# A two-branch linear attention kernel: the low parts of the folded weights move to VectorE, the output weights are split in other places, and the second fold's transposes stand later

## The chip, the cores and the metric

The kernel runs on one core of a Trainium2 chip. The metric is the device time of one execution in microseconds; lower is better. The kernel before takes 364.24 us (median of three runs, 363.75 to 364.63). The core's engines are named as in the profile: PE (TensorE, matrix products), PEld (its weight loads), DVE (VectorE), ACT (ScalarE), POOL (GpSimd) and SP (SyncE, which here only issues transfers).

## The reference

Two attention branches A and B read the same input `x` (2048 tokens, 448 channels, 16 heads of 28), and a per-token gate mixes their outputs. Each branch has weights of its own. Cut to what matters:

```python
q, k, v = split(x @ wqkv)                       # per head, 28 wide
pq, pk = q @ w_phi[h], k @ w_phi[h]             # per head, 28x28
phi_q = concat([softmax(pq), softmax(-pq)])     # 56 features
phi_k = concat([softmax(pk), softmax(-pk)])
kv, z = phi_k.T @ v, phi_k.sum(tokens)
o = (phi_q @ kv) / (phi_q @ z + 1e-6)
branch = o @ wo
out = g * branch_A + (1 - g) * branch_B         # g = sigmoid(x @ gate_w)
```

## The kernel before

**Arithmetic.** All large products are float32 made of two float32r parts: a matrix w is kept as a high part (w rounded by a copy on ACT) and a low part (w minus the high part, a subtraction). A projection of 256 tokens is then 22 matmuls (`proj`, L221). The `w_phi` of each head is folded into the weights of q and k beforehand, so that one projection gives `pq` or `pk`.

**The fold of branch B.** `load_strips` brings the raw weights in, heads on partitions; `fold_strips(1, ...)` multiplies them on PE by `w_phi` (L182) into two PSUM tiles, transposes these on DVE (L186), stores them to a DRAM buffer `td` (four transfers, L188) and loads them back in the wanted layout (three transfers, L191 and L193). `high_folded` then makes the high part on ACT (L200) and `low_folded` the low part (L204), which was POOL's. It is done twice: for the k weights (staged in `wtb[1]`, result `wkb`), and for the q weights (staged in `ctr`, result `wka`, whose space A's k weights leave).

**The output weights.** `wo` of both branches is seven chunks, 0 to 6. `load_wo(c)` brings a chunk from a DRAM copy `wos` into one half of `wtb[0]` or `wtb[1]` (L455), `high_wo(c)` (ACT, L134) and `low_wo(c)` (POOL, L137) split it, and two transfers store the parts in `wod` (L464, L465), from which they come back much later. `wo_part(c)` says where a chunk is staged, and the table `WOS` at which step it is split.

**Order.** The order on each engine is the order in which the program is written: the engines run their own queues in order and wait for each other by semaphores. The first loop has eight steps u of 256 tokens and does A's k and v: a k projection; on DVE the sums of the step before (`k_sums`: L251, L252; the normalisation is POOL's, L260); `k_shift` (DVE L235 to L237, then POOL L238); a v projection, whose result ACT moves out (`v_out`, L268); the exponentials (`k_exp`, ACT L242); and `kv_acc(u - 1)` on PE (L285), which needs the normalised features of the step before. In between stand A's first q projections (`q_front`, DVE L312 and L314, through DRAM buffers `qd` to tiles `tq`; `q_exp0`, `q_min`, `q_exp1` on ACT L337, DVE L341 with POOL L345, ACT L352; `q_turn`, DVE L355), both folds of B and the splitting of `wo`. The second loop has eight steps u, each with one q projection, one k and one v projection of B, `num` (PE L367) and `kv_acc`; `a_turn` (DVE L568) takes the two PSUM tiles of `num` out. At its step 0, `gates` turns the gate sums into a sigmoid (ACT L558, DVE L559 and L560).

**PSUM.** `two_tile()` deals out three tiles in turn (`two0`, `two1`, `two2`), two of them to a fold or to `num`; a projection waits until the tile's last reader is done.

The end of the first loop's step, as it matters here:

```python
        if u == 5:
            low_folded(wtb[1], wk[1], nc.gpsimd)
            load_wo(2, 3, 6)
            ...
            wtqb = load_strips(mid.tile([P, 2048], F32, name="ctr"), wqt[1])
        if u > 1:
            kv_acc(u - 1)
```

Of the kernel before, what the change touches and what calls it, by code (L numbers as in the profile page):

```python
# [15 lines left out]
S, D, H, DH = 2048, 448, 16, 28  # L16
# [33 lines left out]
def hedgehog_mix(ctx: ExitStack, tc: tile.TileContext, xd, wv, wkt, wqt, wphi, wo, cmask, cpmask, out):  # L50


    nc = tc.nc
# [28 lines left out]
    wtb = [res.tile([P, 2048], F32, name=f"wtb{i}") for i in range(2)]  # L82
# [64 lines left out]
    def two_tile(i=None):  # L147
        if i is None:
            i = turn[0] = (turn[0] + 1) % 3
        return twos[i].tile([P, 2, 512], F32, name=f"two{i}")  # L150
# [23 lines left out]
            nc.sync.dma_start(w[HP * r:HP * r + DH, :, :D], s[r][:, :, :D])  # L174
        return dst

    def fold_strips(b, wt, i):
        w, t = wt.rearrange("p (g c) -> p g c", g=4), wt[:, :4 * D]
        ts = [two_tile(), two_tile()]
        for g in range(4):  # L180
            for r in range(4):
                nc.tensor.matmul(ts[r // 2][HP * g:HP * g + HP, r % 2, :D], wps[HP * r:HP * r + DH, b, g],  # L182
                                 w[HP * r:HP * r + DH, g, :D], start=True, stop=True)
        o = t.rearrange("p (j i w m) -> p i w j m", i=2, w=2, m=HP)
        for j, ps in enumerate(ts):
            nc.vector.transpose(o[:, j], ps[:, :, :D].rearrange("p w (j m) -> p w j m", m=HP))  # L186
        for g in range(4):
            nc.sync.dma_start(td[i][:, g * P:g * P + P].rearrange("(j t) x -> t j x", t=HP),  # L188
                              t[HP * g:HP * g + HP].rearrange("t (j x) -> t j x", x=P))
        d = wt.rearrange("p (c x) -> p c x", c=4)  # L190
        nc.sync.dma_start(d[:, :3], td[i][:384].rearrange("(c p) x -> p c x", p=P))  # L191
        for p in (0, 64):
            nc.sync.dma_start(d[p:p + 64, 3], td[i][384:])  # L193
# [4 lines left out]
    def high_folded(wt, dst):  # L198
        w, d = folded(wt, dst)
        nc.scalar.activation(d[0], w, AF.Copy)  # L200

    def low_folded(wt, dst, eng):
        w, d = folded(wt, dst)
        eng.tensor_tensor(d[1], w, d[0].bitcast(F32), OP.subtract)  # L204
# [7 lines left out]
    def proj(u, w, ps, order=None):  # L212
        n = w.shape[3]
        for i, j in order or [(i, j) for i in range(2) for j in range(11)]:
            if i is None:
                warm(j)
                continue
            t = 2 * u + i
            x, o = xg[t // 4], (t % 4) * P
            xc, k, wc = TERMS[j]  # L220
            nc.tensor.matmul(ps[:, i, :n], x[:, xc, o:o + P], w[:, k, wc], start=j == 0, stop=j == 10)  # L221
        return ps
# [66 lines left out]
    def state_copy(b):  # L289
        nc.scalar.activation(kvs[b][:, :, :, :DH], kvp[b].rearrange("p g s f -> p s g f"), AF.Copy)  # L290
# [57 lines left out]
    def q_min(k):  # L348
        q_rest(k, q_least(k))

    def q_exp1(k):
        nc.scalar.activation(eq[:, 1, :, :, :DH], eq[:, 1, :, :, :DH], AF.Exp)  # L352

    def q_turn(k):
        nc.vector.transpose(wtb[k % 2], eq.rearrange("p s a c f -> p (s a c f)"))  # L355
        eTs[k] = wtb[k % 2].rearrange("p (s g t) -> p s g t", s=2, g=4)
# [64 lines left out]
    wt = load_wt(wtb[0], wkt[0], 2)  # L421
# [6 lines left out]
    def warm(n):  # L428
        for i in range(n):
            nc.tensor.transpose(pw[:, 0, :P], ident, ident)  # L430
# [16 lines left out]


    def wo_part(c):
        t = wtb[c in (2, 3)]  # L450
        return [t[:, D * i:D * i + D] for i in (c % 2, 2 + c % 2)]

    def load_wo(*cs):
        for c in cs:
            nc.sync.dma_start(wo_part(c)[0], wos[:, HP * c:HP * (c + 1), :])  # L455
# [10 lines left out]


    WVS = {2: (0, 1), 3: (2, 3)}
    WOS = {3: (0, 1), 5: (4, 5), 6: (2, 3, 6)}
    FRONTS = {2: 0, 5: 1}  # L470
    pq = None
    for u in range(NU):

        if u in (2, 4):
            split_x(u // 2 + 1, 0, 4, 0)
        for c in WVS.get(u, ()):
            high_wv(1, c)
        if u == 5:
            high_folded(wtb[1], wk[1])
            nc.gpsimd.memset(eq[:, :, :, :, DH:], 0.0)  # L480
            for b in range(2):
                nc.gpsimd.memset(kvs[b], 0.0)
        if pq is not None:
            q_front(FRONTS[u - 1], pq)
            q_load(FRONTS[u - 1])
            pq = None
        pk = proj(u, wk[0], two_tile())
        if u > 1:
            k_sums(u - 1)
        if u in (2, 4):  # L490
            split_x(u // 2 + 1, 0, 4, 1)
        k_shift(u, pk)
        if u == 1:
            fold(wtqa, wq[0])
            k_sums(0)
        if u == 2:
            pq = proj(0, wq[0], two_tile())
            kv_acc(0)
        if u > 1:
            pv = proj(u, wvs[0], two_tile())  # L500
            v_out(u, pv)
        k_exp(u)

        if u == 0:
            wtqa = load_wt(wtb[0], wqt[0])
            load_x(2, 0, 4)
            for c in range(0, 4, 2):
                load_wv(1, c)
        if u == 1:
            load_strips(wtb[1], wkt[1])  # L510
            for r in range(4):
                nc.sync.dma_start(wps[HP * r:HP * r + DH], wphi[DH * r:DH * r + DH])
            nc.sync.dma_start(wos.rearrange("g (a f) n -> g a (f n)", f=DH),
                              wo.rearrange("(a g f) n -> g a (f n)", g=4, f=DH))
        if u in (2, 4):
            split_x(u // 2 + 1, 0, 4, 2)
        for c in WVS.get(u, ()):
            low_wv(1, c, nc.gpsimd)
        for c in WOS.get(u, ()):
            high_wo(c)  # L520
            low_wo(c)
        if u == 2:
            load_wo(0, 1)
            load_x(3, 0, 4)
        if u == 4:
            load_wo(4, 5)
        if u == 5:
            low_folded(wtb[1], wk[1], nc.gpsimd)
            load_wo(2, 3, 6)
            start.close()  # L530
            mid = ctx.enter_context(tc.tile_pool(name="mid", bufs=1, side="right"))
            wtqb = load_strips(mid.tile([P, 2048], F32, name="ctr"), wqt[1])
        if u > 1:
            kv_acc(u - 1)
        if u == 3:
            fold_strips(1, wtb[1], 0)
        if u == 7:
            fold_strips(1, wtqb, 1)
        if u == 5:
            pq = proj(FRONTS[u], wq[0], two_tile())  # L540
        if u == 6:
            q_exp0(0)
            q_min(0)
            q_exp1(0)
        if u == 7:
            q_turn(0)
# [29 lines left out]
    for u in range(NU):  # L576
        k = NU + u
        f, m, n = u + 2, u + 1, u - 1
        if u == 2:
            ctr[1] = mid.tile([P, 2048], F32, name="ctr")  # L580
        pq = proj(f % NU, wq[f // NU], two_tile())
        if n >= 0:
            a_turn(n)
            n_rec(n)
        q_exp0(m)
        q_min(m)
        q_exp1(m)
        if n >= 0:
            n_den(n)
            weights(n, nc.gpsimd)  # L590
            if u > 1:
                n_mul(n)
        else:
            k_sums(k - 1)
        q_front(f, pq)
        q_load(f)
        pk = proj(u, wk[1], two_tile())
        if u == 0:
            kv_acc(k - 1)
            state_copy(0)  # L600
        else:
            k_sums(k - 1)
            if u == 1:
                n_mul(n)
        k_shift(k, pk)
        if u == 0:
            state_turn(0)
            q_turn(m)
        pv = proj(u, wvs[1], two_tile())
        v_out(k, pv)  # L610
        k_exp(k)
        if u == 0:
            high_folded(wtqb, wq[1])
            low_folded(wtqb, wq[1], nc.gpsimd)
        else:
            q_turn(m)
        if u == NU - 1:
            woh, wol = [wp_.tile([P, 7, D], F32R, name=n) for n in ("wkb", "wvb")]
            for w, d in ((woh, wod[0]), (wol, wod[1])):
                nc.sync.dma_start(w.bitcast(F32), d)  # L620
        if n >= 0:
            a_add(n)
        if u == 4:
            nc.gpsimd.tensor_scalar(gate[:, 1], gate[:, 0], -1.0, 1.0, op0=OP.mult, op1=OP.add)
        ts = nums[u] = [two_tile(), two_tile()]
        num(u, [t[:, i] for t in ts for i in range(2)])
        if u == 0:
            gates()
        else:
            kv_acc(k - 1)  # L630
# [261 lines left out]
```

## Time and profile before

| | |
|---|---|
| median of three runs | 364.24 us |
| profiled execution | 364.21 us, of which 362.4 us from first to last instruction |
| mean granted TensorE clock | 0.986 of full speed |
| PE busy | 344.9 us (95%) |
| DVE busy | 274.2 us (76%) |
| POOL busy | 269.9 us (74%) |
| ACT busy | 121.7 us (34%) |

A row of the timeline gives the start and the length of a group of equal instructions in microseconds, the engine, the line, the operation, what it writes and reads, the count, and in brackets the engine's idle time before it with what ended that. A row of waits gives the engine and line that waited, what it waited for, the total, the number of times and the longest. A row of the groups gives the total busy time and the mean in nanoseconds.

### The profile page before, as it was taken

Reading aid. Unit: us, or ns where it says so; the run is one execution under the profiler, and the core shown is the slowest. Engines: PE = TensorE matmul, PEld = TensorE weight load, DVE = VectorE, ACT = ScalarE, POOL = GpSimd, SP = SyncE. Lnnn points to the kernel's source line nnn. Section 1 sums busy time; section 2 is a strip of 40 time slices with the busy share of each in tenths; the row PEclk is TensorE's granted clock in tenths of the full one; section 3 lists DMA queues with packets and bytes.
Section 4 is the critical chain, followed back from the end, with each engine's and each line's share of the span. In section 5 each row is a group of like instructions: output and inputs, shape, how many; then the busy total and the mean of one; then the engine's idle time right before and its main releaser. Section 6 shows DMA issues by size and latency. Waiting matters only on the chain.

```text
span 362.4 us, 8503 instructions
## 1 busy us (share of the span) xinstructions
PE 344.9 (95%) x3599; PEld 301.9 (83%) x3599; DVE 274.2 (76%) x313; ACT 121.7 (34%) x170; POOL 269.9 (74%) x230
## 2 busy tenths in 40 slices
PE   8999999999949795999999999999999999999995
PEld 7999888889837684898988889898878978888894
DVE  4328765466635939979989898989899999989740
ACT  5515335242342250133141431312213454534330
POOL 2453899897672535799988897886779999999850
PEclk9999999999987998999999999999999999999999
DMA  8795245853636720322423133229573362564111
GB/s 235 232 327 140 113 117 166 200 163 127 142 77 217 198 83 9 103 81 74 126 79 101 55 103 101 101 78 380 165 248 104 127 174 86 164 192 127 53 51 51
DMA packets 38958, 49.58 MB, mean 137 GB/s; under 512 B 11784, under 2 KB 32104, under 8 KB 38632
## 3 DMA queue, kind: packets, MB, share of 16 engines
q1 hardware_dynamic: 33768, 44.90, 41.5%
q10 hardware_dynamic: 5152, 4.13, 3.6%
q8 instruction: 28, 0.46, 0.5%
q14 instruction: 10, 0.08, 0.1%
HBM read 29.27 MB, written 21.36 MB: 140 GB/s over the span
## 4 chain that ended last, share of the span: by engine, by line
PE 80%; DVE 6%; DMA 5%; POOL 4%; issue 3%; ACT 1%; SPq 1%; POOLq 0%; DVEq 0%; ACTq 0%
PE two L221 51%; PE out L821 16%; PE two L367 5%; PE kv L285 3%; DMA wtb<-wos 3%; PE two L154 2%; POOL e L260 2%; PE two L430 2%; DMA wod<-wtb 1%; POOL wkb L204 1%; DVE glog L559 1%; PE kv L367 1%; DVE wtb L355 1%; DVE wva L752 1%; DVE qmn L341 1%
## 5 line engine op out<-in xcount | busy, mean ns | idle before, releaser
L221 PE MATMUL two<-wka,xg 128*128 128x448 f32 x352 | 73.8, 366 | 0.0
L221 PEld LDWEIGHTS two<-wka,xg 128*128 128x128 f32 x352 | 65.1, 188 | 6.4 <-issue 0.8
L260 POOL TENSOR_TENSOR e<-e,rs 128x896 f32<-128x896 f32 x32 | 53.8, 1703 | 15.0 <-DVE rs L252 15.0
L268 ACT ACTIVATE vs<-two 128x896 f32<-128x896 f32 x16 | 14.7, 918 | 86.5 <-PE two L221 81.1
L221 PE MATMUL two<-wkb,xg 128*128 128x448 f32 x176 | 38.3, 374 | 3.7 <-DVE wva L568 3.7
L221 PEld LDWEIGHTS two<-wkb,xg 128*128 128x128 f32 x176 | 34.3, 195 | 6.6 <-DVE wva L568 4.1
L251 DVE TENSOR_REDUCE sm<-e 128x32 f32<-128x896 f32 x32 | 33.0, 1073 | 8.6 <-ACT e L242 8.6
L221 PE MATMUL two<-wva,xg 128*128 128x450 f32 x176 | 39.4, 374 | 0.0
L221 PE MATMUL two<-wqa,xg 128*128 128x448 f32 x176 | 38.2, 372 | 0.0
L221 PE MATMUL two<-wvb,xg 128*128 128x448 f32 x176 | 37.2, 366 | 0.0
L221 PEld LDWEIGHTS two<-wqa,xg 128*128 128x128 f32 x176 | 32.8, 190 | 4.8 <-ACT e L242 1.5
L355 DVE STREAM_TRANSPOSE wtb<-xrb 128x2048 f32<-128x2048 f32 x16 | 36.6, 2289 | 0.3 <-issue 0.3
L345 POOL TENSOR_TENSOR xrb<-qmn,tq 128x896 f32<-128x896 f32 x16 | 28.2, 1760 | 10.5 <-ACT xrb L337 7.9
L242 ACT ACTIVATE e<-e 128x896 f32<-128x896 f32 x32 | 28.7, 945 | 21.8 <-POOL e L238 21.7
L221 PEld LDWEIGHTS two<-wva,xg 128*128 128x128 f32 x176 | 33.3, 190 | 2.9
L221 PEld LDWEIGHTS two<-wvb,xg 128*128 128x128 f32 x176 | 33.0, 188 | 2.8
L821 PE MATMUL out<-wkb,e 128*128 128x448 f32 x154 | 34.6, 369 | 0.1
L238 POOL TENSOR_TENSOR e<-mx,e 128x896 f32<-128x896 f32 x16 | 27.2, 1702 | 9.6 <-DVE mx L237 9.4
L821 PEld LDWEIGHTS out<-wkb,e 128*128 128x128 f32 x154 | 28.6, 188 | 4.0 <-issue 0.8
L405 POOL TENSOR_TENSOR wva<-wva,cdd 128x896 f32<-128x896 f32 (+1 forms) x12 | 26.5, 2209 | 0.8
L405 POOL TENSOR_TENSOR ctr<-ctr,cdd 128x896 f32<-128x896 f32 (+1 forms) x12 | 26.5, 2211 | 0.6
L352 ACT ACTIVATE xrb<-xrb 128x896 f32<-128x896 f32 x16 | 15.2, 951 | 35.0 <-POOL xrb L345 35.0
(113 smaller groups left out, 588.5 us busy)
## 6 DMA issues: line engine op xcount, KB each, us to landing
tq<-qd SPq DMA_DIRECT2D x16, 448.0 KB
qd<-uq ACTq DMA_DIRECT2D x32, 112.0 KB
qd<-uq SPq DMA_DIRECT2D x32, 112.0 KB
od<-wva SPq DMA_DIRECT2D x8, 448.0 KB
wqa<-od SPq DMA_DIRECT2D x8, 448.0 KB
wod<-wtb SPq DMA_DIRECT2D x14, 224.0 KB
xrb<-in_xt SPq DMA_DIRECT2D x2, 1024.0 KB
out<-bd SPq DMA_DIRECT2D x8, 224.0 KB
```

Of the source, the lines that this page charges most:

```text
L221: nc.tensor.matmul(ps[:, i, :n], x[:, xc, o:o + P], w[:, k, wc], start=j == 0, stop=j == 10)
L238: nc.gpsimd.tensor_tensor(e5[:, 1], mx[:, 1, :, :, None].to_broadcast([P, 2, H, DH]), e5[:, 0], OP.subtract)
L242: nc.scalar.activation(es[k][:, s], es[k][:, s], AF.Exp)
L251: nc.vector.tensor_reduce(sm[:, s], e[:, s].rearrange("p (h f) -> p h f", f=DH), AX.X, OP.add)
L260: nc.gpsimd.tensor_tensor(e3, e3, rs[:, s, :, None].to_broadcast([P, HA, DH]), OP.mult)
L268: nc.scalar.activation(v[:, :, :, :, :DH].rearrange("p w j q f -> p w (j q) f"), hb(ps[:, :, :D]), AF.Copy)
L345: nc.gpsimd.tensor_tensor(eq[:, 1, :, :, :DH], mn.rearrange("p c a -> p a c")[:, :, :, None].to_broadcast([P, 8, 4, DH]), tview(k), OP.sub ...
L352: nc.scalar.activation(eq[:, 1, :, :, :DH], eq[:, 1, :, :, :DH], AF.Exp)
L355: nc.vector.transpose(wtb[k % 2], eq.rearrange("p s a c f -> p (s a c f)"))
L367: nc.tensor.matmul(banks[r][32 * g:32 * g + 32, 256 * s:256 * s + 256], kvt[b][32 * r:32 * r + 32, s, g], eT[32 * r:32 * r + 32, s, g], st ...
L405: nc.gpsimd.tensor_tensor(c3, c3, dd.to_broadcast([P, 8, hi - lo, DH]), OP.mult)
L821: nc.tensor.matmul(outs[t % 2][:, :D], (hi, lo)[x][:, c], w[:, c], start=x == 0 and n == 0 and c == 0, stop=x == 1 and c == 6)
```

## The change

1. The k fold's `high_folded` and `low_folded` are written at the end of step 4 of the first loop (before: the high part at the start of step 5, the low part at its end), and the low part is a DVE instruction.
2. Chunk 6 is staged in `wtb[1]`; chunks 4, 5, 2 and 3 are loaded together at step 4 and split at step 5, chunk 6 alone is loaded at step 5 and split at step 6.
3. `fold_strips` gives its PSUM tiles back, and the transposes with all that follows are a function `turn_strips`. For the q fold it is called in step 0 of the second loop, behind `q_exp0(1)` and `q_min(1)`.
4. The q fold's `high_folded` stands behind `state_copy(0)` in step 0 of the second loop (before: behind `k_exp`), and its `low_folded`, on DVE, behind `q_turn(1)`.

```diff
-    def fold_strips(b, wt, i):
+    def fold_strips(b, wt):
...
+        return ts
+
+    def turn_strips(wt, ts, i):
+        t = wt[:, :4 * D]
         o = t.rearrange("p (j i w m) -> p i w j m", i=2, w=2, m=HP)
         for j, ps in enumerate(ts):
             nc.vector.transpose(o[:, j], ps[:, :, :D].rearrange("p w (j m) -> p w j m", m=HP))
...
-        t = wtb[c in (2, 3)]
+        t = wtb[c // 2 % 2]
...
-    WOS = {3: (0, 1), 5: (4, 5), 6: (2, 3, 6)}
+    WOS = {3: (0, 1), 5: (4, 5, 2, 3), 6: (6,)}
...
         if u == 5:
-            high_folded(wtb[1], wk[1])
...
         if u == 4:
-            load_wo(4, 5)
+            high_folded(wtb[1], wk[1])
+            low_folded(wtb[1], wk[1], nc.vector)
+            load_wo(4, 5, 2, 3)
         if u == 5:
-            low_folded(wtb[1], wk[1], nc.gpsimd)
-            load_wo(2, 3, 6)
+            load_wo(6)
...
         if u == 7:
-            fold_strips(1, wtqb, 1)
+            pf = fold_strips(1, wtqb)
...
         q_exp0(m)
         q_min(m)
+        if u == 0:
+            turn_strips(wtqb, pf, 1)
         q_exp1(m)
...
             state_copy(0)
+            high_folded(wtqb, wq[1])
...
             q_turn(m)
+            low_folded(wtqb, wq[1], nc.vector)
         pv = proj(u, wvs[1], two_tile())
         v_out(k, pv)
         k_exp(k)
-        if u == 0:
-            high_folded(wtqb, wq[1])
-            low_folded(wtqb, wq[1], nc.gpsimd)
-        else:
+        if u > 0:
             q_turn(m)
```

Line numbers behind the edit of `fold_strips` are four higher in the changed kernel. The first place is DVE between steps 4 and 5 of the first loop. The kernel before, with `mx`, `e`, `sm` and `rs` the tiles of `k_shift` and `k_sums`:

```order
L235 TENSOR_REDUCE mx_742<-two0_711 128x32
L236 TENSOR_TENSOR e_743<-two0_711,mx_742 128x896
L237 TENSOR_REDUCE mx_742<-e_743 128x32
L251 TENSOR_REDUCE sm_837<-e_743 128x32 x2
L252 RECIPROCAL rs_838<-sm_837 128x64
L235 TENSOR_REDUCE mx_844<-two2_814 128x32
```

The changed kernel there:

```order
L239 TENSOR_REDUCE mx_742<-two0_711 128x32
L240 TENSOR_TENSOR e_743<-two0_711,mx_742 128x896
L241 TENSOR_REDUCE mx_742<-e_743 128x32
L208 TENSOR_TENSOR wkb_146<-wtb1_124,wkb_146 128x1792
L255 TENSOR_REDUCE sm_840<-e_743 128x32 x2
L256 RECIPROCAL rs_841<-sm_840 128x64
L239 TENSOR_REDUCE mx_847<-two2_817 128x32
```

The low part of `wkb` stands ahead of the sums of step 4, on whose reciprocal POOL's normalisation and then `kv_acc(4)` wait.

The second place is POOL in steps 5 to 7 of the first loop. The kernel before, with `e_845` and `e_993` the features of steps 5 and 6:

```order
L137 TENSOR_TENSOR wtb0_123<-wtb0_123 128x448 x2
L204 TENSOR_TENSOR wkb_146<-wtb1_124,wkb_146 128x1792
L260 TENSOR_TENSOR e_845<-e_845,rs_986 128x896 x2
L238 TENSOR_TENSOR e_993<-mx_992,e_993 128x896
L137 TENSOR_TENSOR wtb1_124<-wtb1_124 128x448 x2
L137 TENSOR_TENSOR wtb0_123<-wtb0_123 128x448
L345 TENSOR_TENSOR xrb_125<-qmn_1070,tq0_131 128x32x28
L260 TENSOR_TENSOR e_993<-e_993,rs_1098 128x896 x2
```

The changed kernel there:

```order
L137 TENSOR_TENSOR wtb0_123<-wtb0_123 128x448 x2
L137 TENSOR_TENSOR wtb1_124<-wtb1_124 128x448 x2
L264 TENSOR_TENSOR e_848<-e_848,rs_994 128x896 x2
L242 TENSOR_TENSOR e_1001<-mx_1000,e_1001 128x896
L137 TENSOR_TENSOR wtb1_124<-wtb1_124 128x448
L349 TENSOR_TENSOR xrb_125<-qmn_1070,tq0_131 128x32x28
L264 TENSOR_TENSOR e_1001<-e_1001,rs_1098 128x896 x2
```

Between the features of step 5 and those of step 6 POOL now has one chunk of `wo` (6) and not three (2, 3, 6); ahead of step 5's it has four chunks and no low part of `wkb`. On SP the transfer that loads chunk 6 stands behind the eight stores of chunks 4, 5, 2 and 3, still ahead of the strips of the q weights.

The third place is ACT in step 0 of the second loop. The kernel before, with `vs` written by `v_out`:

```order
L290 ACTIVATE kvs0_75<-kv_152 128x8x28
L268 ACTIVATE vs0_150<-two1_1310 128x32x28
L242 ACTIVATE e_1301<-e_1301 128x896 x2
L200 ACTIVATE wka_1198<-ctr_893 128x1792
L558 ACTIVATE glog_73<-glog_73 128x16
```

The changed kernel there:

```order
L294 ACTIVATE kvs0_75<-kv_152 128x8x28
L204 ACTIVATE wka_1189<-ctr_901 128x1792
L272 ACTIVATE vs0_150<-two1_1312 128x32x28
L246 ACTIVATE e_1302<-e_1302 128x896 x2
L562 ACTIVATE glog_73<-glog_73 128x16
```

The high part of `wka`, which waits for the last transfers of the q fold, stands ahead of `v_out`, which frees the PSUM tile for the next q projection. On DVE the low part of `wka` stands between `q_turn(1)` (L359 there) and the sigmoid's L563.

More of the change, by code (lines that the diff above doesn't have):

```diff
@@ L175, in load_strips @@
         return dst
-    def fold_strips(b, wt, i):
-        w, t = wt.rearrange("p (g c) -> p g c", g=4), wt[:, :4 * D]
+    def fold_strips(b, wt):
+        w = wt.rearrange("p (g c) -> p g c", g=4)
         ts = [two_tile(), two_tile()]
@@ L535, in hedgehog_mix @@
         if u == 3:
-            fold_strips(1, wtb[1], 0)
+            turn_strips(wtb[1], fold_strips(1, wtb[1]), 0)
         if u == 7:
-            fold_strips(1, wtqb, 1)
+            pf = fold_strips(1, wtqb)
         if u == 5:
```

## The prediction, on record before the changed kernel ran

> **What bounds the kernel now.** I read the page's first part, then what PE waited for, then the timelines of the engines around those waits.
>
> ```profile
> PE 344.9 (95%) x3599; PEld 301.9 (83%) x3599; DVE 274.2 (76%) x313; ACT 121.7 (34%) x170; POOL 269.9 (74%) x230
> ```
>
> ```profile
> PE kv L285 <- POOL e L260: 7.9, 2, 5.2
> PE two L221 <- DVE wva L568: 3.7, 1, 3.7
> ```
>
> PE is the bound nearly everywhere; behind the start it waits three times. PE's timeline has the places, and between rows without a bracket PE does not stop:
>
> ```profile
> 58.44 1.51 PE L182 MATMUL two<-wtb,wps 28*32 28x448 f32 x32
> ...
> 79.19 0.99 PE L285 MATMUL kv<-e,vs 128*29 128x56 f32 x64
> ...
> 109.08 1.72 PE L285 MATMUL kv<-e,vs 128*29 128x56 f32 x64 [5.24 <-POOL e L260]
> ...
> 117.40 4.57 PE L221 MATMUL two<-wkb,xg 128*128 128x448 f32 x22
> 124.59 0.99 PE L285 MATMUL kv<-e,vs 128*29 128x56 f32 x64 [2.62 <-POOL e L260]
> ...
> 130.18 1.49 PE L367 MATMUL two<-wtb,kvt 32*32 32x256 f32 x64
> 131.60 4.75 PE L221 MATMUL two<-wqa,xg 128*128 128x448 f32 x22
> 140.04 6.27 PE L221 MATMUL two<-wkb,xg 128*128 128x448 f32 x22 [3.69 <-DVE wva L568]
> ```
>
> The three waits are `kv_acc(6)`, `kv_acc(7)` and the k projection of step 1: 5.24 + 2.62 + 3.69 = 11.55 us. A wait of over 3 us costs more than itself, because the granted clock (the share before the DMA share) is about half behind it:
>
> ```profile
> 108.00:112.00 4.00, 2.92 (x96) 1.79 (x96) 0.00 (x0) 1.29 (x2) 2.68 (x2) 0.50 0.97 345
> 140.00:144.00 4.00, 3.96 (x12) 3.55 (x13) 3.93 (x6) 0.00 (x0) 1.88 (x3) 0.57 0.08 10
> ```
>
> From 109.08 to 117.40 are 8.32 us for three groups that take 0.99 + 1.51 + 4.57 = 7.07 at full clock: 1.25 us lost. The projection at 140.04 takes 6.27 where the one before it took 4.75: 1.52 lost. The wait of 2.62 has no such loss (0.99 behind it). In all 14.3 us.
>
> What the waits hang on stands on the other engines. POOL:
>
> ```profile
> 75.77 3.37 POOL L260 TENSOR_TENSOR e<-e,rs 128x896 f32<-128x896 f32 x2
> ...
> 97.35 1.16 POOL L137 TENSOR_TENSOR wtb<-wtb 128x448 fp32r<-128x448 f32 x1 [2.42 <-ACT wtb L134]
> ...
> 102.85 1.15 POOL L137 TENSOR_TENSOR wtb<-wtb 128x448 fp32r<-128x448 f32 x1 [1.29 <-ACT wtb L134]
> 103.96 1.75 POOL L345 TENSOR_TENSOR xrb<-qmn,tq 128x896 f32<-128x896 f32 x1
> 105.67 3.35 POOL L260 TENSOR_TENSOR e<-e,rs 128x896 f32<-128x896 f32 x2
> ...
> 134.56 4.00 POOL L204 TENSOR_TENSOR wka<-ctr,wka 128x1792 fp32r<-128x1792 f32 x1 [5.95 <-ACT wka L200]
> ```
>
> ACT, and SP's transfers:
>
> ```profile
> 76.88 1.71 ACT L200 ACTIVATE wkb<-wtb 128x1792 fp32r<-128x1792 f32 x1 [3.59 <-DMA wtb<-td]
> ...
> 94.96 1.79 ACT L242 ACTIVATE e<-e 128x896 f32<-128x896 f32 x2
> 96.66 0.56 ACT L134 ACTIVATE wtb<-wtb 128x448 fp32r<-128x448 f32 x1
> ...
> 102.19 0.58 ACT L134 ACTIVATE wtb<-wtb 128x448 fp32r<-128x448 f32 x1 [1.85 <-DMA wtb<-wos]
> ...
> 130.28 0.92 ACT L268 ACTIVATE vs<-two 128x896 f32<-128x896 f32 x1 [4.28 <-PE two L221]
> 131.11 1.77 ACT L242 ACTIVATE e<-e 128x896 f32<-128x896 f32 x2
> 132.78 1.69 ACT L200 ACTIVATE wka<-ctr 128x1792 fp32r<-128x1792 f32 x1
> ```
>
> ```profile
> 71.19 1.15 SPq L193 DMA_DIRECT2D wtb<-td  x2
> ...
> 89.46 1.70 SPq L455 DMA_DIRECT2D wtb<-wos  x3
> ...
> 93.78 2.56 SPq L321 DMA_DIRECT2D qd<-uq  x2
> 106.48 0.34 SPq L329 DMA_DIRECT2D tq<-qd  x1
> ...
> 121.70 1.13 SPq L193 DMA_DIRECT2D ctr<-td  x2
> ```
>
> DVE, then rows of its groups:
>
> ```profile
> 60.14 2.11 DVE L186 STREAM_TRANSPOSE wtb<-two 128x896 f32<-128x896 f32 x2 [3.76 <-PE two L182]
> ...
> 72.48 2.08 DVE L251 TENSOR_REDUCE sm<-e 128x32 f32<-128x896 f32 x2 [4.49 <-ACT e L242]
> 74.59 0.55 DVE L252 RECIPROCAL rs<-sm 128x64 f32<-128x64 f32 x1
> ...
> 112.76 2.12 DVE L186 STREAM_TRANSPOSE ctr<-two 128x896 f32<-128x896 f32 x2 [10.07 <-DMA wod<-wtb]
> ...
> 134.60 3.99 DVE L559 TENSOR_SCALAR glog<-glog 128x16 f32<-128x16 f32 x1 [5.64 <-ACT glog L558]
> ...
> 138.80 2.31 DVE L568 STREAM_TRANSPOSE wva<-two 128x1024 f32<-128x1024 f32 x2
> ```
>
> ```profile
> L236 DVE TENSOR_TENSOR e<-two,mx 128x896 f32<-128x896 f32 x16 | 17.5, 1092 | 2.4 <-PE kv L285 1.8
> ...
> L137 DVE TENSOR_TENSOR wva<-wvr,wva 128x450 fp32r<-128x450 f32 x4 | 3.1, 824 | 3.9 <-ACT wva L134 3.9
> L439 DVE TENSOR_SCALAR bd<-wp,mask 112x112 f32<-112x112 f32 x4 | 1.1, 331 | 0.0
> ```
>
> The reader is to see that the first wait is POOL's row of chunks 2, 3 and 6 (the last of them lands at 102.19) ahead of the normalisation at 105.67; the second is DVE's transposes of the q fold, late at 112.76 for the first, ahead of the sums of step 7; the third is L559, which takes 3.99 us for 16 columns beside POOL's L204.
>
> **The change, part by part**, in the profiled execution's time (364.21 us; the median is 0.03 above).
>
> *A new wait at `kv_acc(4)`: +7.8.* DVE's low part of `wkb` now stands ahead of the sums of step 4, and it needs ACT's high part, whose input lands at 76.88: nothing in the change makes it land earlier. The high part ends at 78.59. No row has this subtraction on DVE; two of L236 (896 columns, 1.09) give 2.18, L137's rate (824 ns for 450, beside a busy POOL) 3.3, and half of L236's time 1.1. I take 2.18: L236 is the same operation, and POOL stands idle here, its next work waiting for these very sums. Then 80.77; the sums and the reciprocal 2.66 (72.48 to 75.14), 83.43; the normalisation 3.37, 86.8; with four handovers 87.0. PE did this at 79.19 without a wait. So 7.8 us (6.7 to 8.9). `k_shift(5)`, queued behind on DVE, ends near 86.7, before the exponentials that ACT can then do, and the k projection of step 6 does not reach its tile before.
>
> *The clock behind it: +1.4*, between the two losses measured above (1.25 and 1.52); zero would need the clock to stay up through 7.8 us, and both longer waits show it down. From here PE is 9.2 us later than before.
>
> The Trainium skill's page "TensorE: Matmul & The Clock Gate", section "What's actually happening", lets PE run at half clock for about 3.4 us of work after an idle window. By that the loss would be 1.7, and the time 360.7.
>
> *The wait at `kv_acc(6)`: −5.24 and −1.25.* PE gets there at 103.84 + 9.2 = 113.0. POOL's way: L260 of step 4 to 87.0, L238 as long as L345, which has its size, 1.75, ACT's exponentials 1.79 to 90.5, four chunk copies of 0.56 and POOL's four of 1.15 to 95.7, which stays ahead of step 5's sums (they follow the q projection of step 1). The exponentials of step 6 ended at 96.75, now 105.95; chunk 6 then takes 0.58 on ACT and 1.15 on POOL, L345 1.75, L260 3.35: 112.8. No wait, with 0.2 to spare, if chunk 6 has landed by 105.95. SP issues it behind the stores of 4, 5, 2 and 3 and a store's landing, near 97.4: it has 8.5 us. Of the three loads at 89.46, the first was there at 96.66 without a wait (at most 6.6 from its issue), the last took 11.0, with two others ahead of it. Here it is the first of its group, so I take the first; the last is the range's end. Chunks 2 and 3, issued at 80.8, have ten microseconds until ACT comes to them.
>
> *The wait at `kv_acc(7)`: −2.62.* The fold's matmuls end at 115.5, the transposes at 117.6, sums 120.3, normalisation 123.7; PE gets there at 124.65. `q_turn(0)` and `q_min(1)`, now ahead of the transposes, run from about 110.5 to 114 while DVE has nothing else, if `tq` has landed.
>
> *A new wait at the q projection of step 1: +1.3.* ACT's high part of `wka` now stands ahead of `v_out`, so what follows it includes the exponentials, the gates and the PSUM tile. Before, the transposes ended at 114.88 and the last load's issue at 122.83; in the first fold the landing came 4.54 behind that issue (72.34 to 76.88), so 12.5 us from transposes to landing; the first fold itself took 14.6 (62.25 to 76.88). With 12.5: 130.1, the copy 131.8, `v_out` 132.8, handovers 132.9. PE is through `num` (1.42) at 131.6. So 1.3; with 14.6 it is 3.4, and with a faster landing nothing. I take the second fold's own rows.
>
> *The wait at the k projection of step 1: −3.69 and −1.52.* The low part of `wka` ends at 134.0; `v_out`, the exponentials and L558 bring DVE's L559 to 134.7. L559 ended at 138.59 and L204 beside it at 138.56, and L439, with seven times the columns, takes 0.33: I take 0.33 for it with POOL idle, then 0.55 for the reciprocal (L252's, which has four times the columns), 1.16 for the first transpose: 136.8. PE comes at 137.5.
>
> Row L559 taken alone, 3.99 us, would give 140.4 and a wait of 2.9: 363.3. The Trainium skill's page "SBUF — State Buffer", section "SBUF: two separate sides", has VectorE in a two-port mode, or with two SBUF inputs, and GpSimd exclude each other for a whole instruction. By that the 3.99 was POOL's lock, and the sum stays 360.4.
>
> POOL's two subtractions of 4.0 that go, and the low parts' other readers, have POOL and DVE idle around them and cost nothing more; steps 2 to 7 and the output are PE's and move as they are.
>
> Sum: 7.8 + 1.4 + 1.3 − 6.49 − 2.62 − 5.21 = −3.8, so 360.4.
>
> **Rivals.** *Late transfers, mildly.* If chunk 6 takes the 11.0 us of the last load, POOL is 2.5 late, less 0.2: 362.7. The same crowd can hold `tq`: its stores took until 106.48 from 93.78, and `q_min(1)` would then hold the transposes by up to 2.8: 363.2. For it: POOL had to wait for each chunk. Against: two chunks fewer in the crowd.
>
> *The other side: chunk 6 very late.* Chunk 6 has its own load only after a store's landing, with the strips of the q weights on its heels. The stores of `qd` needed over 12.4 us in this stretch; at 12.4 the wait at `kv_acc(6)` is 3.7 and takes the clock down again (1.4): 365.5. From about 12.1 us on the kernel is slower. Against: everything behind chunk 6 is issued later than it.
>
> *L559 keeps its 4 us:* 363.3, as above; its own row speaks for it, L439 and the common end with L204 against.
>
> *The new wait doesn't come,* because DVE's part finds its input earlier: then 351 us. Against: the landing at 76.88 has the same issues ahead of it in both orders.
>
> **Chances.** What a measurement here can tell from no change is about 0.2%, 0.7 us. The forecast, 358.9 to 361.9: 0.64; mildly late transfers, 0.18; L559, 0.05; chunk 6 very late, 0.08; the missing wait, 0.02; something else, 0.03, shared evenly. The range 358.9 to 363.2 leaves about two in ten out. Faster 0.82, same 0.09, slower 0.09: of the late transfers and L559 about a third lands within 0.2%.
>
> **What would show it.** `kv_acc(4)` near 87.0 behind a wait of 7 to 9 us on POOL's normalisation, and a low clock behind it; DVE idle for some ten microseconds until 78.6; the waits at `kv_acc(6)` and `kv_acc(7)` gone or under 0.5; the q projection of step 1 waiting 1 to 3 us for ACT; L559 under 0.5 us and no wait behind it. I am wrong if chunk 6's copy on ACT waits for its load, or if the wait at `kv_acc(4)` is not there.

## The result and the profile after

| | before | after |
|---|---|---|
| median | 364.29 us (363.75 to 364.63, four runs) | 361.36 us (360.93 to 362.25, four runs) |
| profiled execution | 364.21 us, span 362.4 | 361.31 us, span 359.5 |
| mean granted TensorE clock | 0.986 | 0.984 |
| POOL busy | 269.9 us | 261.9 us |

The ratio is 0.9924, with a 95% interval of 0.9902 to 0.9947: 2.9 us faster, where 3.8 had been forecast. What PE waited for in the changed kernel (engine, line, releaser, total, times, longest):

```profile
PE kv L289 <- POOL e L264: 7.7, 1, 7.7
PE two L225 <- ACT vs L272: 2.1, 1, 2.1
```

Behind the start, three waits have become two. PE's timeline has their places:

```profile
87.01 1.72 PE L289 MATMUL kv<-e,vs 128*29 128x56 f32 x64 [7.68 <-POOL e L264]
88.66 6.16 PE L225 MATMUL two<-wqa,xg 128*128 128x448 f32 x22
...
113.69 0.99 PE L289 MATMUL kv<-e,vs 128*29 128x56 f32 x64
114.62 1.05 PE L182 MATMUL two<-ctr,wps 28*32 28x448 f32 x32
...
120.19 4.57 PE L225 MATMUL two<-wkb,xg 128*128 128x448 f32 x22
124.69 0.99 PE L289 MATMUL kv<-e,vs 128*29 128x56 f32 x64
...
133.96 4.76 PE L225 MATMUL two<-wqa,xg 128*128 128x448 f32 x22 [2.08 <-ACT vs L272]
138.56 4.57 PE L225 MATMUL two<-wkb,xg 128*128 128x448 f32 x22
142.96 4.63 PE L225 MATMUL two<-wvb,xg 128*128 128x448 f32 x22
```

The same stretch of the kernel before has two rows on the way from `kv_acc(6)` to the k projection that the prediction did not show, and the v projection of step 1:

```profile
110.72 1.81 PE L182 MATMUL two<-ctr,wps 28*32 28x448 f32 x32
112.46 5.10 PE L221 MATMUL two<-wqa,xg 128*128 128x448 f32 x22
...
146.15 4.63 PE L221 MATMUL two<-wvb,xg 128*128 128x448 f32 x22
```

Starts read side by side give a ledger of how late (+) or early (−) PE is against the kernel before: `kv_acc(4)` 79.19 to 87.01, +7.8; `kv_acc(6)` 109.08 to 113.69, +4.6; the k projection of step 0 117.40 to 120.19, +2.8; `kv_acc(7)` 124.59 to 124.69, +0.1; the q projection of step 1 131.60 to 133.96, +2.4; the k projection 140.04 to 138.56, −1.5; the v projection 146.15 to 142.96, −3.2. About 0.3 is given back later: 0.2 of it before `kv_acc` of step 2 (168.05 to 165.03, −3.0), the rest near the end.

DVE, ACT and POOL around these places:

```profile
78.86 2.03 DVE L208 TENSOR_TENSOR wkb<-wtb,wkb 128x1792 fp32r<-128x1792 f32 x1 [10.65 <-ACT wkb L204]
...
112.56 2.30 DVE L359 STREAM_TRANSPOSE wtb<-xrb 128x2048 f32<-128x2048 f32 x1
...
115.89 2.11 DVE L190 STREAM_TRANSPOSE ctr<-two 128x896 f32<-128x896 f32 x2
...
135.72 0.17 DVE L563 TENSOR_SCALAR glog<-glog 128x16 f32<-128x16 f32 x1 [0.56 <-ACT glog L562]
```

```profile
77.12 1.71 ACT L204 ACTIVATE wkb<-wtb 128x1792 fp32r<-128x1792 f32 x1 [3.62 <-DMA wtb<-td]
...
106.61 0.56 ACT L134 ACTIVATE wtb<-wtb 128x448 fp32r<-128x448 f32 x1
...
131.41 1.70 ACT L204 ACTIVATE wka<-ctr 128x1792 fp32r<-128x1792 f32 x1 [5.30 <-DMA ctr<-td]
133.01 0.90 ACT L272 ACTIVATE vs<-two 128x896 f32<-128x896 f32 x1
```

```profile
83.60 3.35 POOL L264 TENSOR_TENSOR e<-e,rs 128x896 f32<-128x896 f32 x2 [7.58 <-DVE rs L256]
...
120.70 3.37 POOL L264 TENSOR_TENSOR e<-e,rs 128x896 f32<-128x896 f32 x2 [2.97 <-DVE rs L256]
```

The reader is to see DVE idle for 10.65 us until ACT's high part is there at 78.86, and POOL's normalisation at 83.60 waiting for the sums behind it; chunk 6 copied at 106.61 without a wait for its load; ACT's eviction of v (L272) held behind the high part of `wka`; and the gates' addition (L563, the one added in the sigmoid), 3.99 us before, at 0.17 with POOL idle.

### The profile page after: what moved, and what is told of

Its sections match the earlier page's. It is cut to its first block, busy times and chain, and to the rows that moved or that the text cites. A ratio compares the mean times of both kernels' runs of the same rounds, so it can differ in the third digit from the quotient of the medians.

```text
span 359.5 us, 8502 instructions
## 1 busy us (share of the span) xinstructions
PE 343.5 (96%) x3599; PEld 301.2 (84%) x3599; DVE 275.1 (77%) x315; ACT 121.4 (34%) x170; POOL 261.9 (73%) x228
## 4 chain that ended last, share of the span: by engine, by line
PE 72%; DMA 8%; POOL 7%; DVE 7%; ACT 2%; issue 1%; SPq 1%; POOLq 0%; ACTq 0%; DVEq 0%
PE two L225 45%; PE out L826 16%; PE two L371 4%; PE kv L289 3%; POOL e L264 3%; DMA wtb<-wos 2%; PE two L154 2%; DMA ctr<-td 2%; DMA wtb<-td 1%; DMA xrb<-in_xt 1%; DMA td<-wtb 1%; DVE sm L255 1%; POOL wva L409 1%; SPq L192 1%; PE kv L371 1%
## 5 line engine op out<-in xcount | busy, mean ns | idle before, releaser
L272 ACT ACTIVATE vs<-two 128x896 f32<-128x896 f32 x16 | 14.7, 918 | 84.4 <-PE two L225 84.4
L225 PE MATMUL two<-wqa,xg 128*128 128x448 f32 x176 | 39.3, 380 | 2.1 <-ACT vs L272 2.1
L225 PEld LDWEIGHTS two<-wqa,xg 128*128 128x128 f32 x176 | 33.7, 195 | 6.5 <-ACT vs L272 2.6
L359 DVE STREAM_TRANSPOSE wtb<-xrb 128x2048 f32<-128x2048 f32 x16 | 36.6, 2288 | 0.0
L225 PE MATMUL two<-wkb,xg 128*128 128x448 f32 x176 | 36.6, 363 | 0.0
L255 DVE TENSOR_REDUCE sm<-e 128x32 f32<-128x896 f32 x32 | 33.0, 1072 | 4.2 <-ACT e L246 4.2
L225 PEld LDWEIGHTS two<-wkb,xg 128*128 128x128 f32 x176 | 33.0, 188 | 2.3
L316 DVE TENSOR_REDUCE qmx<-two 128x32 f32<-128x896 f32 x14 | 15.0, 1073 | 16.0 <-PE two L225 16.0
```

The lines of the kernel that those rows point to most:

```text
L255: nc.vector.tensor_reduce(sm[:, s], e[:, s].rearrange("p (h f) -> p h f", f=DH), AX.X, OP.add)
L272: nc.scalar.activation(v[:, :, :, :, :DH].rearrange("p w j q f -> p w (j q) f"), hb(ps[:, :, :D]), AF.Copy)
L316: nc.vector.tensor_reduce(mx, p4, AX.X, OP.max)
```

## The experiments

Each is set against runs of the kernel before on the same chip. A difference in microseconds between kernels that ran on different chips is taken through these ratios. A trace is of one execution, and its time is named where it lies far from the median.

**e1: the low part of `wkb` behind the reductions of step 5.** In the changed kernel the subtraction is written behind `k_shift(5)`, with the loads of chunks 2 and 3 behind it.

```diff
         k_shift(u, pk)
+        if u == 5:
+            low_folded(wtb[1], wk[1], nc.vector)
+            load_wo(2, 3)
...
             high_folded(wtb[1], wk[1])
-            low_folded(wtb[1], wk[1], nc.vector)
-            load_wo(4, 5, 2, 3)
+            load_wo(4, 5)
```

> As the changed kernel, but the k fold's low part stands on DVE behind step 5's k_shift, not ahead of step 4's sums; chunks 2 and 3 of the output weights are loaded behind it. Theory (the 7.7 us wait at kv_acc(4) is DVE standing in order behind ACT's high part): the wait goes, and the low clock behind it (2.1 us) with it. Chunk 6 is then ready about 1 us too late for kv_acc(6), and the wait for ACT at step 1's q projection grows by about half a us. 353 to 354 us. Rival (the wait is the price of the fold itself and comes back at kv_acc(5), because POOL has chunks 2 and 3 ahead of step 5's normalisation, which land later): a wait of 5 us or more at kv_acc(5) or kv_acc(6), 358 to 361 us.

Measured: 355.57 us, ratio 0.9721 (0.9651 to 0.9792). Its profiled execution was a long one (358.98; the other three took 354.53 to 356.49), so its waits may be larger than usual. PE there:

```profile
79.31 0.99 PE L289 MATMUL kv<-e,vs 128*29 128x56 f32 x64
...
95.75 0.99 PE L289 MATMUL kv<-e,vs 128*29 128x56 f32 x64 [1.83 <-POOL e L264]
...
108.27 1.72 PE L289 MATMUL kv<-e,vs 128*29 128x56 f32 x64 [2.43 <-POOL e L264]
...
130.22 6.29 PE L225 MATMUL two<-wqa,xg 128*128 128x448 f32 x22 [2.48 <-ACT vs L272]
```

The wait at `kv_acc(4)` is gone, so the place of one DVE instruction made it. The wait and its clock had cost 9.8 us; the medians gain 5.8 and the ratios 7.4. New waits behind POOL's chunk copies, and the slow projection behind the wait for ACT (6.29 instead of 4.76), took part of the rest, and the median stayed above the 353 to 354 expected. At `kv_acc(6)` PE now comes 7.85 us earlier than in the changed kernel (105.84 for 113.69), and a wait of 2.43 stands there again.

The same trace has a subtraction on DVE beside one on POOL; the rows are DVE's and POOL's timelines:

```profile
79.48 3.32 DVE L208 TENSOR_TENSOR wkb<-wtb,wkb 128x1792 fp32r<-128x1792 f32 x1 [1.04 <-ACT wkb L204]
```

```profile
79.21 1.70 POOL L242 TENSOR_TENSOR e<-mx,e 128x896 f32<-128x896 f32 x1
```

POOL ended at 80.91; DVE's end at 82.80 is 1.89 later, about the 2.03 that the subtraction takes alone. DVE did its work after POOL, not beside it.

**e2: DVE's low part of `wka` alone,** in the kernel before.

```diff
-            low_folded(wtqb, wq[1], nc.gpsimd)
+            low_folded(wtqb, wq[1], nc.vector)
```

> The kernel before with one word changed: the q fold's low part is DVE's and not POOL's. Theory (L559 took 3.99 us because POOL's subtraction ran beside it): it takes about 0.2 us, the wait at step 1's k projection falls from 3.7 to about 2 us (DVE's subtraction of 2.0 takes the place of the 4), and the clock stays up: 3.3 us faster, 361 us. Rival (L559 takes 4 us by itself): the wait grows to 5.5 us, 366 us.

Measured: 361.94 us, 0.9906 (0.9874 to 0.9939). The profiled execution was the longest of ten (365.25); what it has on top lies ahead of these rows, at `kv_acc(5)` to `kv_acc(7)` and in a slow v projection. DVE's timeline and PE's:

```profile
139.69 0.17 DVE L559 TENSOR_SCALAR glog<-glog 128x16 f32<-128x16 f32 x1
```

```profile
141.31 4.68 PE L221 MATMUL two<-wkb,xg 128*128 128x448 f32 x22 [1.71 <-DVE wva L568]
```

The gates' addition takes 0.17 us once POOL has no subtraction beside it, so the 3.99 was not its own. The wait of 3.69 falls to 1.71 and the projection behind it takes 4.68 instead of 6.27. This one line gives as much as the whole change (0.9924).

**e3: the q fold's half of the change** (points 3 and 4), with the k fold and the output weights as before.

```diff
-            fold_strips(1, wtqb, 1)
+            pf = fold_strips(1, wtqb)
...
+        if u == 0:
+            turn_strips(wtqb, pf, 1)
...
+            high_folded(wtqb, wq[1])
...
+            low_folded(wtqb, wq[1], nc.vector)
...
-            high_folded(wtqb, wq[1])
-            low_folded(wtqb, wq[1], nc.gpsimd)
```

> Only the q fold's half of the change: transposes behind q_min(1), high part ahead of v_out, low part on DVE; the k fold and the loads of the output weights as before. Theory (the two halves' waits add up): the 5.2 us at kv_acc(6) stay with their clock loss, the 2.6 at kv_acc(7) and the 3.7 with 1.5 of clock at step 1's k projection go, a wait of about 2 for ACT at its q projection comes: 358 to 359 us. Rival (the late fold governs, so the transposes gain nothing by standing behind q_min): the 2.6 at kv_acc(7) stay, 361 us.

Measured: 363.87 us, 0.9963 (0.9923 to 1.0004), above both forecasts. PE's and DVE's rows:

```profile
125.09 1.71 PE L289 MATMUL kv<-e,vs 128*29 128x56 f32 x64 [2.37 <-POOL e L264]
```

```profile
113.69 2.31 DVE L359 STREAM_TRANSPOSE wtb<-xrb 128x2048 f32<-128x2048 f32 x1 [11.08 <-DMA wod<-wtb]
...
116.89 2.10 DVE L190 STREAM_TRANSPOSE ctr<-two 128x896 f32<-128x896 f32 x2
```

The wait at `kv_acc(7)` stays. `q_turn(0)` writes `wtb[0]`, where chunk 6 is staged here, and waits for its stores until 113.69; the fold's transposes, now behind it, are later than before, not earlier.

**e4: the other half** (points 1 and 2), with the q fold as before.

```diff
-        t = wtb[c in (2, 3)]
+        t = wtb[c // 2 % 2]
...
-    WOS = {3: (0, 1), 5: (4, 5), 6: (2, 3, 6)}
+    WOS = {3: (0, 1), 5: (4, 5, 2, 3), 6: (6,)}
...
-            high_folded(wtb[1], wk[1])
...
-            load_wo(4, 5)
+            high_folded(wtb[1], wk[1])
+            low_folded(wtb[1], wk[1], nc.vector)
+            load_wo(4, 5, 2, 3)
...
-            low_folded(wtb[1], wk[1], nc.gpsimd)
-            load_wo(2, 3, 6)
+            load_wo(6)
```

> Only the k fold's half of the change: its low part on DVE ahead of step 4's sums, chunks 4, 5, 2, 3 together and 6 alone; the q fold as before. Theory: a wait of 7.7 at kv_acc(4) with 2.1 of clock comes, the 5.2 at kv_acc(6) with 1.8 of clock goes, the other two waits stay at 2.4 and 3.7: 2 to 3 us slower, 366 to 367 us. Rival (the wait at kv_acc(4) takes up slack that the later waits need anyway): within 1 us of the kernel before.

Measured: 367.28 us, 1.0042 (1.001 to 1.0075). PE's and DVE's rows:

```profile
87.39 1.72 PE L285 MATMUL kv<-e,vs 128*29 128x56 f32 x64 [8.24 <-POOL e L260]
...
127.32 0.99 PE L285 MATMUL kv<-e,vs 128*29 128x56 f32 x64 [2.54 <-POOL e L260]
128.24 6.30 PE L221 MATMUL two<-wvb,xg 128*128 128x448 f32 x22
...
144.33 7.01 PE L221 MATMUL two<-wkb,xg 128*128 128x448 f32 x22 [3.67 <-DVE wva L568]
```

```profile
138.90 3.98 DVE L559 TENSOR_SCALAR glog<-glog 128x16 f32<-128x16 f32 x1 [7.22 <-ACT glog L558]
```

By itself this half loses, as the theory had it. By the ratios the halves make +1.5 and −1.3 us, near zero together, where both at once make −2.8; each of the three numbers is uncertain by 0.8 to 1.5. The traces name the main part of these 3 us: the wait at `kv_acc(7)` is in e3 (2.37) and in e4 (2.54), each with slow matmuls behind it, and only with both halves is it gone. The trace of e3 is of a short execution (362.12), that of e4 of its longest (369.38).

**e11: the turns alone.** In the kernel before, the second fold's transposes stand behind `q_min(1)`, nothing else is changed.

```diff
-            fold_strips(1, wtqb, 1)
+            pf = fold_strips(1, wtqb)
...
         q_min(m)
+        if u == 0:
+            turn_strips(wtqb, pf, 1)
         q_exp1(m)
```

> The kernel before with one thing changed: the turns of the second fold stand behind those of q, with both low parts on GpSimd and the output weights as before. The prediction's step: the 2.62 at kv_acc(7) were the turns ahead of step 7's sums, so they go, and the later low part on GpSimd adds 0 to 1 at the k projection of step 1: 361.5 to 363. Rival, as e3 suggests (2.37 left there): while chunk 6 is late, step 7's sums wait for the turn of q behind its stores, with or without the turns; nothing goes at kv_acc(7), the high part of wka lands later, and the k projection of step 1 waits longer: 365 to 367.

Measured: 366.61 us, 1.0053 (1.0027 to 1.0079). DVE's and PE's timelines:

```profile
115.71 2.31 DVE L359 STREAM_TRANSPOSE wtb<-xrb 128x2048 f32<-128x2048 f32 x1 [13.15 <-DMA wod<-wtb]
...
118.91 2.10 DVE L190 STREAM_TRANSPOSE ctr<-two 128x896 f32<-128x896 f32 x2
```

```profile
120.07 7.39 PE L225 MATMUL two<-wkb,xg 128*128 128x448 f32 x22 [2.96 <-DVE ctr L190]
127.39 0.99 PE L289 MATMUL kv<-e,vs 128*29 128x56 f32 x64
```

The time is the rival's, the mechanism neither's. The wait at `kv_acc(7)` goes, but PE waits 2.96 one projection earlier, for the PSUM tile that the untransposed fold still holds, and loses 2.8 more to the clock (7.39 against 4.57). So the new place of the turns alone is a loss. The rows suggest that it gains once chunk 6 no longer holds `q_turn(0)`; no run has points 2 and 3 of the change without the others.

**e5: ScalarE's high part of `wka` behind the eviction of v** in the changed kernel, and VectorE's low part in step 1.

```diff
             state_copy(0)
-            high_folded(wtqb, wq[1])
...
             q_turn(m)
+        if u == 1:
             low_folded(wtqb, wq[1], nc.vector)
...
         v_out(k, pv)
+        if u == 0:
+            high_folded(wtqb, wq[1])
```

> The changed kernel with one thing moved: in step 0 of the second phase ScalarE's high part of wka is written behind the eviction of the v projection instead of ahead of it, and VectorE's low part of wka one step later. Theory: the 2.08 us that TensorE waits at the q projection of step 1 comes from the order on ScalarE alone (the high part, held till 131.41 by the transfer of ctr, stood ahead of the eviction of v at 133.01); the matmuls behind that wait ran at 4.76, so no clock hangs on it. The wait goes and the time falls by about 2.1, to 359.0 to 359.6. Rival: the exponentials and the gates behind the high part become the late ones, and the k projection or the numerators of step 1 wait instead; then it stays at 361 to 361.6.

Measured: 362.34 us, 0.9919 (0.989 to 0.9949): no gain on the changed kernel's 0.9924, against the theory. The wait of 2.08 is gone from PE's waits, and a new row stands there:

```profile
PE two L371 <- DVE e L240: 1.5, 1, 1.5
```

These are the numerators (`num`) of step 2. The low part (147.35, 2.28 us) came in step 1, where DVE has no idle time. The rival's sense holds, at 0.7 above its range.

**e9: the same with the low part in step 0,** right behind the high part.

```diff
+        if u == 0:
+            high_folded(wtqb, wq[1])
+            low_folded(wtqb, wq[1], nc.vector)
         k_exp(k)
```

> e5 with VectorE's low part of wka back in step 0, right behind ScalarE's high part and ahead of the gates. Theory: e5 won the 2.08 at the q projection and gave it back because the 2.28 of the low part stood in step 1, where VectorE has no idle time, so the numerators of step 2 waited 1.5 (and began 0.6 late in step 1). In step 0 VectorE waits 4.18 for the gates' exponential, which hides the low part: 359.2 to 360. Rival: what e5 lost came from ScalarE's later high part, not from the low part's place; then it stays at 361.5 to 362.5.

Measured: 360.71 us, 0.9879 (0.985 to 0.9907), about 1.6 us under the changed kernel by the ratios; the intervals touch. PE waits 0.79 at the k projection and no more at the numerators of step 2. The theory's sign held; the median lies 0.7 over its range.

**e6: chunks 2, 3 and 6 one step later,** on top of e1.

```diff
-    WOS = {3: (0, 1), 5: (4, 5, 2, 3), 6: (6,)}
+    WOS = {3: (0, 1), 5: (4, 5), 6: (2, 3), 7: (6,)}
...
-        if u == 5:
+        if u == 6:
             load_wo(6)
+        if u == 5:
             start.close()
```

> The kernel of e1 (low part of wkb behind the reductions of step 5) with chunks 2 and 3 of the output weights split in step 6 instead of 5, chunk 6 in step 7 instead of 6, and the strips' load ahead of chunk 6's. Theory: what is left in e1 at kv_acc(5) (1.83) and kv_acc(6) (2.43, with 0.7 of clock there and 0.55 in the fold behind it) is GpSimd waiting for ScalarE's high parts of chunks 2 and 3, whose loads landed at 88 and 90.5. With these a step later the loads have over 12 us, the waits go: 5.5 off e1's profiled 359.0, about 353.5; against e1's median 355.6 about 352.5 to 354. Rival: chunk 6 takes their place in step 7, GpSimd's sums of step 7 stand behind it, and kv_acc(7) waits 2 to 4 us: 355.5 to 358.

**e7: e6 with the order of e5.**

```diff
             state_copy(0)
-            high_folded(wtqb, wq[1])
...
+        if u == 1:
             low_folded(wtqb, wq[1], nc.vector)
...
         v_out(k, pv)
+        if u == 0:
+            high_folded(wtqb, wq[1])
```

> e6 with the order of e5 as well. Theory: each wait is paid by itself, so the sum holds: e6 less the 2.48 at the q projection of step 1 and the 1.54 that its matmuls lost to the clock behind it (6.29 instead of 4.75), about 349.5 to 351. Rival: with the start of the second phase earlier by some 8 us the transfers of wqt's strips and of the turned weights come late, and wka is waited for elsewhere: 352 or more.

Measured: e6 355.09 us, 0.9727 (0.9674 to 0.9779); e7 355.65 us, 0.9739 (0.9683 to 0.9795). Neither is clear of e1's 0.9721. In e6 the waits at `kv_acc(5)` and `kv_acc(6)` are gone but for 0.82, and PE pays at the next place instead:

```profile
126.39 6.29 PE L225 MATMUL two<-wqa,xg 128*128 128x448 f32 x22 [3.86 <-ACT vs L272]
```

In e7 that wait is gone, and two others have come:

```profile
129.16 4.68 PE L225 MATMUL two<-wkb,xg 128*128 128x448 f32 x22 [1.74 <-DVE wva L575]
...
156.93 1.45 PE L371 MATMUL two<-wtb,kvt 32*32 32x256 f32 x60 [1.49 <-DVE e L240]
```

Both forecasts were too low, e7's by over 4 us. Its rival gave the time but not the cause: `wka` is not waited for. Waits are not paid one by one here: DVE in steps 0 to 2 is the next to be late, and these two waits make 3.23 of the 3.86 us that went.

**e8: e7 with the k fold's low part back on POOL,** and its high part back at the start of step 5.

```diff
         if u == 5:
+            high_folded(wtb[1], wk[1])
             nc.gpsimd.memset(eq[:, :, :, :, DH:], 0.0)
...
         if u == 5:
-            low_folded(wtb[1], wk[1], nc.vector)
-            load_wo(2, 3)
...
         if u == 4:
-            high_folded(wtb[1], wk[1])
             load_wo(4, 5)
...
         if u == 5:
+            low_folded(wtb[1], wk[1], nc.gpsimd)
+            load_wo(2, 3)
```

> e7 with the k fold's high part back at the top of step 5 and its low part back on GpSimd in step 5 where the kernel before has it (4.05 us there). Theory: in the kernel before GpSimd's 4.05 us made no wait at kv_acc(5) or (4); what made the waits was the transfers behind it, which now have a step more. So VectorE's low part of wkb is worth nothing by itself: within 0.5 us of e7. Rival: GpSimd's load is what bounds steps 5 to 7, and e8 is 2 to 4 us slower than e7.

Measured: 361.73 us, 0.9938 (0.9902 to 0.9975), 6.1 above e7. POOL's row, then PE's:

```profile
85.38 4.06 POOL L208 TENSOR_TENSOR wkb<-wtb,wkb 128x1792 fp32r<-128x1792 f32 x1
```

```profile
106.80 0.99 PE L289 MATMUL kv<-e,vs 128*29 128x56 f32 x64 [2.99 <-POOL e L264]
...
121.43 0.99 PE L289 MATMUL kv<-e,vs 128*29 128x56 f32 x64 [3.57 <-POOL e L264]
```

The rival's side, and more than its 2 to 4: in e7's order VectorE's low part of `wkb`, with the earlier place that it has there, is worth about 6 us. The loads of chunks 2 and 3 wait for it too: SP issues them at 80.95 in e7 and at 89.47 here, and chunk 6 follows at 100.48 and 109.32.

**e10: the gates first.** In e7, ScalarE's high part goes behind the gates' exponential and VectorE's low part behind the first transposes of step 1.

```diff
             a_turn(n)
+            if n == 0:
+                low_folded(wtqb, wq[1], nc.vector)
             n_rec(n)
...
-        if u == 1:
-            low_folded(wtqb, wq[1], nc.vector)
...
-        if u == 0:
-            high_folded(wtqb, wq[1])
...
             gates()
+            high_folded(wtqb, wq[1])
```

> e7 with ScalarE's high part of wka behind the gates' exponential and VectorE's low part right behind the transposes of the first numerators in step 1. Theory: in e7 the gates stood behind the high part (127.31), so the transposes came at 127.92 and the k projection waited 1.74, and the low part at 139.84 made the numerators of step 2 wait 1.49 with 0.6 in step 1. Both go, since VectorE starts its step about 3 us earlier and spends 2 of them on the low part: 3 to 3.8 less than e7's 355.65, 351.8 to 352.7. Rival: VectorE is the bound of steps 1 and 2 whatever the order, and the wait returns one step later: within 1 of 355.6.

Measured: 351.36 us, 0.9632 (0.9605 to 0.966), a little better than the theory and 13.4 below the kernel before. Its two longest totals of waits on PE behind the start, and DVE's rows at the end of step 0:

```profile
PE kv L289 <- POOL e L264: 1.1, 2, 0.9
PE two L225 <- ACT wva L134: 1.0, 1, 1.0
```

```profile
124.89 0.17 DVE L566 TENSOR_SCALAR glog<-glog 128x16 f32<-128x16 f32 x1 [2.46 <-ACT glog L565]
...
125.27 2.31 DVE L575 STREAM_TRANSPOSE wva<-two 128x1024 f32<-128x1024 f32 x2
127.50 1.99 DVE L208 TENSOR_TENSOR wka<-ctr,wka 128x1792 fp32r<-128x1792 f32 x1
```

What others wait for (gates, transposes) now comes first, and the weights that are first read six steps later come behind it. No wait on PE is over 1.3 us (at the start), and none behind it is over 0.9.

## Why the prediction was right, and where its sizes were off

The sign, the six places and the order of their sizes held; 360.4 was 1.0 below the result. Part of that closeness is luck: two losses were sized 0.7 and 0.8 too small and two gains 0.6 and 0.2 too small, so that the errors partly cancel.

- *`kv_acc(4)`, +7.8:* 7.68, shown by e1, where it goes with the instruction's place. The subtraction took 2.03 (2.18 assumed), its input came 0.24 later.
- *The clock behind it, +1.4:* 2.14 (1.72 − 0.99 and 6.16 − 4.75), with the q projection of step 1 the largest error. The windows of the changed kernel, whose PEclk is the number before the DMA share:

```profile
84.00:88.00 4.00, 0.99 (x44) 0.99 (x48) 2.58 (x3) 0.00 (x0) 4.00 (x3) 0.50 0.25 94
88.00:92.00 4.00, 4.00 (x42) 3.52 (x35) 0.00 (x0) 3.35 (x6) 1.63 (x2) 0.53 0.07 23
```

The clock was still low when PE resumed at 87.01 and full only near 91.8 (a mean of 0.53 over the last four microseconds leaves 0.24 us at full speed), so about 4.7 us of work went at half speed. The prediction sized this by two losses behind shorter waits, and read both of these too small, as the next points show.

The Trainium skill's "TensorE: Matmul & The Clock Gate", section "What's actually happening", says that the window is free-running, so that the point of return varies. With its 3.4 us the estimate was 1.7; the measured 2.14 is above that too.

- *`kv_acc(6)`, −5.24 and −1.25:* the wait went, with chunk 6 ready. The clock was worth more: 1.72 − 0.99, 1.81 − 1.05 and 5.10 − 4.75 make 1.84. The prediction took the first fold's 1.51 for the second fold's full-clock time, which is 1.05, and set the lengths of rows that overlap against a difference of starts; together this hid 0.6 of the loss. The gain is also not independent of `kv_acc(4)`: POOL was ready 0.25 us ahead of a PE that came 9.85 later than before (103.84 to 113.69), and in e1, where PE is there at 105.84, 2.43 of wait are left.
- *`kv_acc(7)`, −2.62:* the number held, and the rows came as forecast: the normalisation ended at 124.07 (forecast 123.7), PE got there at 124.69 (124.65). But PE came 2.7 us later than before (121.97), while the normalisation ended only 0.5 earlier (124.53), so the wait went because the sums did not follow a late PE. In e4, with the same late PE and the old order, they follow, and 2.54 are left. The new order has to have an early `q_turn(0)` with it: in e3, where that waits for the stores of the chunks, 2.37 are left, and e11, with the order alone, loses 1.8 us. The prediction credited the order and did not say that `q_turn(0)` needs point 2 of the change. In e1, with points 2 and 3 and PE not late, there is no wait at `kv_acc(7)`. Whether `q_turn(0)` can start early there because of chunk 6's place or because of the fewer stores ahead of it, no run tells apart.
- *The q projection of step 1, +1.3:* 2.08. ACT's copy started 13.4 us after the transposes' end (115.89 + 2.11 to 131.41) where 12.5 was put together from the two folds of the kernel before, and the transposes ended 0.4 later; PE came 0.3 later than forecast and waited that much less.
- *The k projection of step 1, −3.69 and −1.52:* both went. The second was 1.70, since this projection takes 4.57 at full clock and not the 4.75 of the q projection ahead of it. The choice of a short L559 beside an idle POOL was the right one, and e2 shows it apart from the rest.

Measured in the same terms: 7.68 + 2.14 + 2.08 − 5.24 − 1.84 − 2.62 − 3.69 − 1.70 (6.27 − 4.57) = −3.2, which is the ledger's number at the v projection of step 1 (to about 0.2, since the two executions differ by that much ahead of the first place). Of the rivals, late transfers did not come (chunk 6's copy and `q_min(1)` wait for nothing), nor did the others. The border of 12.1 us in the rival with a very late chunk 6 does not follow from that rival's own sum, which with its 1.4 for the clock turns slower near 11.2. Why the 0.3 us behind step 1 is lost was not followed.

## What to carry to other kernels

An instruction moved to a faster engine is first of all moved in a queue: ask what stands behind it there and when its input comes, since here one 2.0 us subtraction ahead of its input's arrival cost 9.8 us, and behind the next reductions no wait at that place. Put work whose result is needed late behind everything that others wait for now; the same instructions in that order, with three chunks split a step later, gave 13.4 us instead of 2.9. And the gains of two changes need not add: a wait upstream delays PE and hides waits downstream, and one wait can be held by both, so test them together and apart.

## What the runs showed of the hardware

**VectorE and GpSimd took turns when both had a two-input operation.** The same subtraction on DVE took 2.03 us alone and 3.32 in e1, where POOL's had begun 0.27 us before it. In e6 DVE's began first, and POOL's, 1.70 otherwise, took 3.49. DVE's and POOL's timelines in e6:

```profile
78.43 2.27 DVE L208 TENSOR_TENSOR wkb<-wtb,wkb 128x1792 fp32r<-128x1792 f32 x1 [0.42 <-ACT wkb L204]
```

```profile
78.78 3.49 POOL L242 TENSOR_TENSOR e<-mx,e 128x896 f32<-128x896 f32 x1
```

POOL ended at 82.27, 1.57 us after DVE's 80.70. The gates' addition beside POOL's 4.0 us is the same picture (3.99 and 3.98 against 0.17). DVE's reductions were not held in this way: L251 took 2.07 at 87.10 in the kernel before beside POOL's 4.05, and L255 the same 2.07 at 80.80 in the changed kernel with POOL idle. The Trainium skill's "SBUF — State Buffer", section "SBUF: two separate sides", states the taking of turns as an exclusive lock for a whole instruction, given to whoever starts first, for VectorE in a two-port mode or with two SBUF inputs; the traces agree for the subtractions. The gates' addition has one SBUF input, and no run here tells whether its mode puts it under the rule.

**The clock fell behind some waits of 2.4 to 3.1 us and not behind others.** Behind 2.43 and 2.48 us (e1), 2.37 (e3) and 2.96 (e11) the next matmuls were slow. Behind 2.54 in e4 and 3.09 in e2 `kv_acc(7)` still took 0.99, and the v projection behind it 6.30 instead of 4.74, so the fall can come about a microsecond after PE has resumed; e8 shows the same behind 3.57 (6.27). Behind 2.99 (e8, at `kv_acc(6)`), 2.62 (the kernel before), 2.08 (the changed kernel) and 1.83 (e1) nothing was slow. So length alone does not decide it in this range, and the prediction's "over 3 us" is no border; what else decides was not tested.
